# Narrowing 64-bit weight words on Trainium2: three instructions a block instead of four, with the sign carried by ScalarE's Prelu

## The chip, the core and the metric

The kernel runs on one core of one Trainium2 chip. A core has five engines with a queue of instructions each: TensorE (PE) for matrix products, VectorE (DVE), ScalarE (ACT) and GpSimd (POOL) for work on tiles, and SyncE (SP), which here issues the DMA transfers. Each engine takes its queue in order: an instruction that waits holds up all that stand behind it on the same engine. The metric is device time in microseconds of one execution; less is better.

## The reference

Three layers in a row, all in fp32 for the reader, with weights that reach the chip as 64-bit words (float64):

```
attention: B 4, H 8, S 576, D 64; a key is seen if 0 <= i - j < 64
x  = softmax(q k^T / 8, masked) v          -> 2304 x 512
g  = x @ w_gate; h1 = silu(g) * (x @ w_val)     512 -> 1536
x2 = h1 @ w_out                                1536 -> 512
h2 = (x2 @ w1) * (x2 @ w2)                      512 -> 1024
out = (h2 @ w3) @ w_out2                       1024 -> 1024 -> 512
```

## The kernel before

**Stages.** Attention takes 24 steps (about 10 to 107 us of the profiled execution); a step takes two groups of queries: S on PE (L400, L410), the maxima on DVE (L417), two groups of three Exp on ACT (L424), the reciprocal of the sums on DVE (L430, L431), the scaling on POOL (L434), the transposition on PE (L443) and its copy on DVE (L449), then P times V on PE (L463) and its copy on ACT (L477, L480). Stages follow each other in one program: the first gate (w_gate, w_val; to about 387), project (w_out, L691 ff., to about 540), the second gate (w1, w2; to about 717) and the final products.

**Matrix products.** Every operand is split in a high and a low part, and a product takes three passes (high x high, high x low, low x high). The gates multiply blocks of 768 tokens by seven products instead of eight; their weight operands (w_g_1h and so on) and token operands (xo_10 and so on) are sums of blocks, made by casts (L197), subtractions (L201) and combinations (L205). Project goes over three token parts of 768 (tp); in each over twelve blocks f of 128 rows of w_out; for every second f it needs two casts ph and two subtractions pl, of h that was stored to memory and loaded back. At the end of a tp, ACT and DVE copy the accumulators to X (L721, L724), which frees them for the next tp.

**Narrowing.** A load brings 128 x 1024 words of 64 bits into a tile `st` (two buffers: a third load waits for the first tile to be read). `narrow` (L176 to L193) makes an fp32 number of each word, 512 columns at a time, in four jobs: a (L185, DVE) shifts the low word right by 29; b (L187, DVE) takes the sign bit of the high word and joins it to that; c (L189, ACT) multiplies the high word, read as a float, by 2^-112, which moves its exponent to the range of fp32; d (L191, DVE) shifts the high word left by three and joins the low word. There are 38 loads, so 76 blocks. What follows makes operands of them, or (w_out, w_out2, w3) copies them (by_wo, by_z, by_w) for a store to memory (wo, zd, w3d), from which they are loaded again in fp32. The copies by_z and by_w share two buffers: a copy waits for the store before the last one.

**Order.** Nothing is scheduled at run time. A class `Plan` (L86 to L150) holds a list of jobs, each with the engines that may do it, a cost for each, and the jobs it needs. While the fixed work of a stage is written out, `advance` lets the plan's clock go on and puts each job on an engine's queue where its own reckoning finds a free time: a job can start when those that it needs are reckoned done. A load is reckoned landed `plan.landing` = 6.0 us after its issue (10.0 in the first two f of project). In attention, `during_attention` charges a step's fixed work as 2.9 us of DVE, 3.2 of ACT and 2.6 of POOL and then advances by 3.85. POOL takes no jobs after attention. SP's loads stand in the same kind of queue, and SP keeps eight transfers under way: the ninth is issued when one of them has landed.

Of the kernel before, what the change touches and what calls it, by code (L numbers as in the profile page):

```python
# [7 lines left out]
F32 = mybir.dt.float32  # L8
# [3 lines left out]
AF = mybir.ActivationFunctionType  # L12
ALU = mybir.AluOpType
# [19 lines left out]
def window_attention_moe_kernel(ctx: ExitStack, tc: tile.TileContext, q, k, v, w_gate, w_val, w_out, w1, w2, w3, w_out2, out):  # L33
# [118 lines left out]
    plan = Plan()  # L152
# [8 lines left out]
    def act(n):  # L161
        return 0.17 + 0.0009 * n

    def dve(n):
        return 0.16 + 0.00104 * n
# [6 lines left out]
    def halves(t):  # L172
        words = t.bitcast(I32).rearrange("p (n two) -> p n two", two=2)
        return words[:, :, 0], words[:, :, 1]

    def narrow(part, load):  # L176

        def low():
            return halves(part())[0]

        def high():
            return halves(part())[1]

        n = 512
        a = plan.job(lambda eng: eng.tensor_scalar(out=low(), in0=low(), scalar1=29, scalar2=None,  # L185
                                                   op0=ALU.logical_shift_right), [load], DVE=0.1 + 0.0006 * n)
        b = plan.job(lambda eng: eng.scalar_tensor_tensor(out=low(), in0=high(), scalar=-2 ** 31, in1=low(),  # L187
                                                          op0=ALU.bitwise_and, op1=ALU.bitwise_or), [a], DVE=dve(n))
        c = plan.job(lambda eng: eng.mul(out=high().bitcast(F32), in_=high().bitcast(F32), mul=2.0 ** -112),  # L189
                     [b], ACT=act(n))  # L190
        return plan.job(lambda eng: eng.scalar_tensor_tensor(out=high(), in0=high(), scalar=3, in1=low(),  # L191
                                                             op0=ALU.logical_shift_left, op1=ALU.bitwise_or),
                        [c], DVE=dve(n))  # L193

    def cast(hi, src, after, n, slots=1):
        def fn(eng):
# [17 lines left out]
    class Doubles:  # L214
# [15 lines left out]
        def narrowed(self):  # L230
            return [narrow(lambda j=j: self.st[:, 512 * j:512 * j + 512], self.loaded) for j in range(2)]
# [848 lines left out]
```

## Time and profile before

| | us |
|---|---|
| runs | 873.64, 871.74, 873.38 |
| median | 873.38 |
| span of the profiled execution, first to last instruction | 869.7 |
| PE busy | 839.7 (97%) |
| DVE busy | 582.2 (67%) |
| ACT busy | 421.2 (48%) |
| POOL busy | 86.2 (10%) |

The span is that of one profiled execution; of that execution the profile has the span alone, and the median of the runs is 3.7 us above it. A profile is read by stretch here: PE is busy nearly all the time, and the others are busy at other times, so the shares of the whole say little. Where PE stands idle, the row after the gap names who released it.

### The profile page before, as it was taken

What the parts mean: (1) busy time and instruction counts of PE and PEld (TensorE: products, weight loads), DVE (VectorE), ACT (ScalarE), POOL (GpSimd) and SP (SyncE); (2) the same over time, 40 slices, a digit from 0 to 9 for tenths busy, and PEclk for the clock granted to TensorE, in tenths of its full rate; (3) what the DMA queues carried; (4) which work ended last, traced back from release to release, by engine and by line L of the source; (5) the groups of instructions that cost most, each with busy time, mean ns of one, the idle gap of its engine ahead of it and who ended that gap; (6) DMA issues with size and microseconds to landing.
All of it is one profiled execution on the core that took longest, in us unless ns stands there. A gap on an engine that the chain in (4) does not pass through costs nothing.

```text
span 869.7 us, 14819 instructions
## 1 busy us (share of the span) xinstructions
PE 839.7 (97%) x5610; PEld 791.1 (91%) x5610; DVE 582.2 (67%) x1173; ACT 421.2 (48%) x1075; POOL 86.2 (10%) x119
## 2 busy tenths in 40 slices
PE   7899888899999999999989999999999999999998
PEld 6777687899999999999989999999999998888886
DVE  4899958878688768875797573867788644531400
ACT  6878855464646454733465442445454423430300
POOL 3678930000000000000000000000000000000000
PEclk9999999999999999999999999999999999999999
DMA  9979300135356323599987331023545179131511
GB/s 198 218 159 188 93 1 37 40 126 189 111 186 219 124 104 151 200 350 402 369 300 245 119 122 49 37 71 123 194 158 193 50 267 362 39 131 64 179 49 48
DMA packets 112535, 136.23 MB, mean 157 GB/s; under 512 B 61392, under 2 KB 78032, under 8 KB 111440
## 3 DMA queue, kind: packets, MB, share of 16 engines
q1 hardware_dynamic: 112320, 135.16, 47.6%
q8 instruction: 44, 0.72, 0.4%
q14 instruction: 27, 0.22, 0.1%
q10 hardware_dynamic: 144, 0.13, 0.0%
HBM read 92.27 MB, written 42.99 MB: 156 GB/s over the span
## 4 chain that ended last, share of the span: by engine, by line
PE 81%; DVE 7%; DMA 5%; ACT 2%; SPq 2%; issue 1%; POOL 1%; POOLq 0%; ACTq 0%; DVEq 0%
PE ala L578 14%; PE alb L578 14%; PE o L707 12%; PE out L818 11%; PE beb L578 7%; PE bea L578 7%; PE acc L774 5%; PE gab L578 3%; PE gaa L578 3%; DMA wo<-wo 2%; DMA zd<-by_z 2%; PE PV L463 1%; DVE ptt L449 1%; SPq L347 1%; DMA st_z<-in_moe_w_out_dram 1%
## 5 line engine op out<-in xcount | busy, mean ns | idle before, releaser
L707 PE MATMUL o<-ph,wo 128*128 128x384 f32 x576 | 147.7, 337 | 2.7 <-ACT X L721 2.7
L707 PEld LDWEIGHTS o<-ph,wo 128*128 128x128 f32 x576 | 105.0, 189 | 3.0 <-ACT X L721 3.0
L707 PE MATMUL o<-pl,wo 128*128 128x384 f32 x288 | 96.9, 336 | 0.0
L585 ACT COPY ha<-ala 128x384 f32<-128x384 f32 x90 | 42.9, 479 | 51.5 <-PE ala L578 50.3
L589 DVE TENSOR_TENSOR ha<-ha,bea 128x384 f32<-128x384 f32 x60 | 33.2, 553 | 45.0 <-PE bea L578 26.6
L707 PEld LDWEIGHTS o<-pl,wo 128*128 128x128 f32 x288 | 54.5, 189 | 0.0
L424 ACT ACTIVATE pexp<-S,stat 128x128 f32<-128x128 f32 x144 | 51.8, 392 | 0.0
L599 ACT ACTIVATE ha<-ha 128x384 f32<-128x384 f32 x54 | 28.4, 526 | 39.0 <-DVE ha L589 39.0
L434 POOL TENSOR_TENSOR pexp<-pexp,stat 128x384 f32<-128x384 f32 x48 | 44.4, 945 | 28.5 <-DVE stat L431 22.6
L836 DVE COPY o<-out 128x512 f32<-128x512 f32 x11 | 7.6, 692 | 57.7 <-PE out L818 57.7
L201 DVE TENSOR_TENSOR pl<-pl,ph 128x768 fp32r<-128x768 f32 x36 | 33.5, 956 | 16.5 <-ACT ph L197 16.1
L197 ACT CAST ph<-pl 128x768 fp32r<-128x768 f32 x36 | 29.3, 835 | 31.1 <-DMA pl<-h 24.1
L585 ACT COPY c12b<-alb 128x384 f32<-128x384 f32 x30 | 14.5, 482 | 48.7 <-PE alb L578 48.6
L833 ACT COPY o<-out 128x512 f32<-128x512 f32 x6 | 3.5, 588 | 65.5 <-PE out L818 65.5
L589 DVE TENSOR_TENSOR c22b<-c22b,beb 128x384 f32<-128x384 f32 x30 | 16.6, 554 | 26.4 <-ACT c22b L585 26.3
L424 ACT ACTIVATION_READ_ACCUMULATOR pexp<-S,stat 128x1 f32 x144 | 33.1, 230 | 0.0
L417 DVE TENSOR_REDUCE stat<-S 128x3 f32<-128x384 f32 x48 | 24.3, 546 | 8.2 <-PE S L410 8.0
L463 PEld LDWEIGHTS PV<-ptt,v 128*64 128x64 f32 x576 | 19.5, 137 | 10.2 <-DVE ptt L449 5.7
L463 PE MATMUL PV<-ptt,v 128*64 128x64 f32 x576 | 22.9, 227 | 6.1 <-DVE ptt L449 5.0
L578 PE MATMUL ala<-xo,w_g_1h 128*128 128x384 f32 x120 | 26.9, 337 | 1.7 <-ACT w_g_1h L197 1.7
L201 DVE TENSOR_TENSOR xo<-X,xo 128x384 fp32r<-128x384 f32 x37 | 22.6, 641 | 5.7 <-ACT xo L197 5.7
L201 DVE TENSOR_TENSOR fl<-fl,fh 128x768 fp32r<-128x768 f32 x24 | 21.7, 952 | 6.9 <-ACT fh L197 6.9
(490 smaller groups left out, 2407.4 us busy)
## 6 DMA issues: line engine op xcount, KB each, us to landing
h<-ha SPq DMA_DIRECT2D x60, 384.0 KB, 3.2
pl<-h SPq DMA_DIRECT2D x36, 384.0 KB, 6.7
fl<-h SPq DMA_DIRECT2D x24, 384.0 KB, 6.1
st_w<-in_moe_w_dram SPq DMA_DIRECT2D x8, 1024.0 KB, 6.9
st_g<-in_moe_w_gate_dram SPq DMA_DIRECT2D x6, 1024.0 KB, 5.5
st_v<-in_moe_w_val_dram SPq DMA_DIRECT2D x6, 1024.0 KB, 5.4
st_wo<-in_moe_w_out_dram SPq DMA_DIRECT2D x6, 1024.0 KB, 5.8
wo<-by_wo SPq DMA_DIRECT2D x12, 512.0 KB, 3.9
```

What stands on the lines that cost most here:

```text
L197: (eng.copy if eng is nc.scalar else eng.tensor_copy)(out=hi(), in_=src())
L201: return plan.job(lambda eng: eng.tensor_tensor(out=lo(), in0=src(), in1=hi().bitcast(F32), op=ALU.subtract), after, slots=slots, DVE=dve( ...
L424: nc.scalar.activation(out=pe[:, jj, :], in_=so[:, jj, :], func=AF.Exp, bias=st[:, 0, x, jj:jj + 1], accum_out=st[:, 1, x, jj:jj + 1])
L434: nc.gpsimd.tensor_tensor(out=pe, in0=pe, in1=st[:, 3, x, :].unsqueeze(2).to_broadcast([P, SUB, P]), op=ALU.mult)
L463: nc.tensor.matmul(pp[64 * h:64 * h + 64, 64 * (SUB * x + jj):64 * (SUB * x + jj) + 64], lhsT=vt[u][e][:, at, h, :], rhs=t[:, x, jj, c:c + ...
L578: nc.tensor.matmul(acc, lhsT=self.wt.ops[p, x][:, m, :], rhs=self.xs.ops[p, m][:, y, :], start=start and n == 0, stop=n == 5, skip_group_c ...
L585: nc.scalar.copy(out=out, in_=src)
L589: nc.vector.tensor_tensor(out=out, in0=x, in1=y, op=ALU.add)
L599: nc.scalar.activation(out=h, in_=src, func=func)
L707: nc.tensor.matmul(acc[m, x], lhsT=wos.tiles[i // 6][:, i % 6, :], rhs=rows[2 * tp + x].words(f, b), start=f == n == 0, stop=f == NF - 1 a ...
L774: nc.tensor.matmul(acc, lhsT=w3T[i][c // 3][:, x, (c % 3) * P:(c % 3) * P + P], rhs=zt[c, y], start=c == n == 0, stop=c == NI - 1 and n == 2)
L818: nc.tensor.matmul(acc, lhsT=rows[blk].words(i, x)[:, t * P:t * P + P], rhs=w34[i][y], start=i == n == 0, stop=i == NI - 1 and n == 2)
```

## The change

Job b no longer works on DVE and no longer waits for a. It is one Prelu on ACT, on the high word read as a float: the word is multiplied by 2^-112, and where it is negative also by -2^32, which makes it positive and puts 32 into its exponent. The last shift left by three then moves that exponent bit to the place of the sign. Job d needs both a and b. So the multiplication (c) and the join of the sign (b on DVE) become one instruction on ACT.

```
-        b = plan.job(lambda eng: eng.scalar_tensor_tensor(out=low(), in0=high(), scalar=-2 ** 31, in1=low(),
-                                                          op0=ALU.bitwise_and, op1=ALU.bitwise_or), [a], DVE=dve(n))
-        c = plan.job(lambda eng: eng.mul(out=high().bitcast(F32), in_=high().bitcast(F32), mul=2.0 ** -112),
-                     [b], ACT=act(n))
+        b = plan.job(lambda eng: eng.activation(out=high().bitcast(F32), in_=high().bitcast(F32), func=AF.Prelu,
+                                                scale=2.0 ** -112, alpha=-2.0 ** 32), [load], ACT=act(n))
         return plan.job(lambda eng: eng.scalar_tensor_tensor(out=high(), in0=high(), scalar=3, in1=low(),
                                                              op0=ALU.logical_shift_left, op1=ALU.bitwise_or),
-                        [c], DVE=dve(n))
+                        [a, b], DVE=dve(n))
```

Since the plan reckons with other costs and other needs, jobs of all kinds come to stand at other places. Three places on ACT follow; the numbers in a name tell tiles of one kind apart, and differ between the programs for the same tile.

ACT in attention, from the Exp of one step to those of the next, before (st_g is the first weight tile, stat the step's maxima and sums, pexp the Exp):

```order
L424 ACTIVATE pexp_456,stat_443<-S_387,stat_443 128x128 x3
L424 ACTIVATE pexp_517,stat_443<-S_389,stat_443 128x128 x3
L385 ACTIVATE qT_531<-T_0_488 128x288
L385 ACTIVATE qT_531<-T_1_492 128x288
L480 COPY X_0_454<-PV_496 128x192
L480 COPY X_1_535<-PV_496 128x192
L424 ACTIVATE pexp_537,stat_521<-S_469,stat_521 128x128 x3
L189 ACTIVATE st_g_310<-st_g_310 128x512
L424 ACTIVATE pexp_601,stat_521<-S_471,stat_521 128x128 x3
L387 COPY kT_615<-T_3_572 128x288
```

and now (st_v is the second weight tile):

```order
L424 ACTIVATE pexp_456,stat_443<-S_387,stat_443 128x128 x3
L189 ACTIVATE st_g_310<-st_g_310 128x512 x2
L424 ACTIVATE pexp_518,stat_443<-S_389,stat_443 128x128 x3
L385 ACTIVATE qT_532<-T_0_489 128x288
L385 ACTIVATE qT_532<-T_1_493 128x288
L480 COPY X_0_454<-PV_497 128x192
L480 COPY X_1_536<-PV_497 128x192
L424 ACTIVATE pexp_538,stat_522<-S_470,stat_522 128x128 x3
L189 ACTIVATE st_v_460<-st_v_460 128x512
L424 ACTIVATE pexp_605,stat_522<-S_472,stat_522 128x128 x3
```

Both steps on st_g moved ahead of a group of Exp in the earlier step, and the first one on st_v, which stood some steps later, came between the two groups of the next.

ACT in project, at the operands of f = 6 (ph_0_3, ph_1_3), before (st_z is a tile of w_out2, by_z its copies):

```order
L189 ACTIVATE st_z_4673<-st_z_4673 128x512 x2
L197 CAST by_z_0_5001<-st_z_4673 128x512
L197 CAST by_z_1_5004<-st_z_4673 128x512
L189 ACTIVATE st_z_4743<-st_z_4743 128x512 x2
L197 CAST ph_0_3_5069<-pl_0_3_4989 128x768
L197 CAST ph_1_3_5072<-pl_1_3_4991 128x768
L197 CAST by_z_0_5076<-st_z_4743 128x512
L197 CAST by_z_1_5078<-st_z_4743 128x512
```

and now:

```order
L197 CAST ph_0_2_4924<-pl_0_2_4779 128x768
L197 CAST ph_1_2_4928<-pl_1_2_4781 128x768
L189 ACTIVATE st_z_4665<-st_z_4665 128x512 x2
L197 CAST by_z_0_4964<-st_z_4645 128x512
L197 CAST by_z_1_4967<-st_z_4645 128x512
L197 CAST by_z_0_5002<-st_z_4665 128x512
L197 CAST ph_0_3_5032<-pl_0_3_4958 128x768
L197 CAST ph_1_3_5035<-pl_1_3_4960 128x768
L197 CAST by_z_1_5039<-st_z_4665 128x512
```

The first copy of the second tile, by_z_0, stood behind ph_0_3 and ph_1_3 and now stands ahead of them.

ACT at the end of project's first token part, before (st_w is a tile of w3, by_w its copies, X the copies of the accumulators):

```order
L197 CAST ph_0_0_5284<-pl_0_0_5208 128x768
L197 CAST ph_1_0_5290<-pl_1_0_5210 128x768
L189 ACTIVATE st_w_5217<-st_w_5217 128x512 x2
L881 COPY by_w_0_5328<-st_w_5217 128x512
L881 COPY by_w_1_5330<-st_w_5217 128x512
L197 CAST ph_0_1_5364<-pl_0_1_5286 128x768
L197 CAST ph_1_1_5366<-pl_1_1_5288 128x768
L721 COPY X_0_0_4921<-o_0_1_4926 128x384
L721 COPY X_0_1_4922<-o_1_1_4928 128x384
```

and now:

```order
L189 ACTIVATE st_w_5142<-st_w_5142 128x512 x2
L197 CAST ph_0_0_5252<-pl_0_0_5173 128x768
L197 CAST ph_1_0_5254<-pl_1_0_5175 128x768
L881 COPY by_w_0_5257<-st_w_5142 128x512
L881 COPY by_w_1_5260<-st_w_5142 128x512
L189 ACTIVATE st_w_5216<-st_w_5216 128x512 x2
L197 CAST ph_0_1_5323<-pl_0_1_5248 128x768
L197 CAST ph_1_1_5326<-pl_1_1_5250 128x768
L881 COPY by_w_0_5329<-st_w_5216 128x512
L881 COPY by_w_1_5332<-st_w_5216 128x512
L721 COPY X_0_0_4885<-o_0_1_4890 128x384
L721 COPY X_0_1_4886<-o_1_1_4892 128x384
```

A second tile of w3 now stands with its narrowing and its copies ahead of the copies X; before, one tile did.

## Rows read from the trace of the kernel before

**Rows 1.** The page, totals of each engine and the line on project's subtraction.
```profile
span 869.7 us, 14819 instructions
...
PE 839.7 (97%) x5610; PEld 791.1 (91%) x5610; DVE 582.2 (67%) x1173; ACT 421.2 (48%) x1075; POOL 86.2 (10%) x119
...
L201 DVE TENSOR_TENSOR pl<-pl,ph 128x768 fp32r<-128x768 f32 x36 | 33.5, 956 | 16.5 <-ACT ph L197 16.1
```

**Rows 2.** Stretches: us; busy PE, PEld, DVE, ACT, POOL; clock, DMA share, GB/s.
```profile
80.00:100.00 20.00, 18.27 (x310) 14.90 (x311) 19.53 (x43) 17.53 (x82) 18.70 (x26) 1.00 0.67 161
180.00:200.00 20.00, 20.00 (x117) 20.00 (x116) 13.49 (x30) 11.20 (x26) 0.00 (x0) 1.00 0.36 127
400.00:420.00 20.00, 20.00 (x117) 20.00 (x116) 11.05 (x17) 7.11 (x10) 0.00 (x0) 1.00 1.04 406
```

**Rows 3.** Waits of PE: who was waited for, us in total, times, longest.
```profile
PE o L707 <- ACT X L721: 2.7, 1, 2.7
...
PE ala L578 <- ACT w_g_1h L197: 1.7, 1, 1.7
...
PE beb L578 <- DVE w_b_3h L201: 0.5, 1, 0.5
```

**Rows 4.** Line 187: duration ns min/median/max, first and last start.
```profile
L187 DVE SCALAR_TENSOR_TENSOR st_g<-st_g x12: 652/686/691, 23.5 to 332.9; 128x512 int32<-128x512 int32 x12
L187 DVE SCALAR_TENSOR_TENSOR st_v<-st_v x12: 684/689/1257, 45.1 to 354.9; 128x512 int32<-128x512 int32 x12
```

**Rows 5.** ACT in order of time: start, us, line, tiles, [idle before].
```profile
27.85 0.39 ACT L424 ACTIVATE pexp<-S,stat 128x128 f32<-128x128 f32 x1
...
49.22 0.70 ACT L189 ACTIVATE st_v<-st_v 128x512 f32<-128x512 f32 x1
```

**Rows 6.** Line 499, ACT's first table load.
```profile
L499 ACT ACT_TABLE_LOAD  x1: 1283/1283/1283, 0.8 to 0.8; - x1
```

**Rows 7.** SP's queue in order of time, around 27 us.
```profile
26.80 0.59 SPq L227 DMA_DIRECT2D st_v<-in_moe_w_val_dram  x1
```

**Rows 8.** DMA issues from 26.5 to 27.2: KB, median us to landing.
```profile
st_v<-in_moe_w_val_dram SPq DMA_DIRECT2D x1, 1024.0 KB, 6.4
```

**Rows 9.** DVE in order of time, in attention.
```profile
29.73 0.16 DVE L430 TENSOR_SCALAR stat<-stat 128x6 f32<-128x6 f32 x1
...
30.36 1.30 DVE L191 SCALAR_TENSOR_TENSOR st_g<-st_g 128x512 int32<-128x512 int32 x1
...
37.42 1.01 DVE L417 TENSOR_REDUCE stat<-S 128x3 f32<-128x384 f32 x2
...
40.87 1.01 DVE L417 TENSOR_REDUCE stat<-S 128x3 f32<-128x384 f32 x2
```

**Rows 10.** PE in order of time, two places where it waited.
```profile
115.48 0.62 PE L578 MATMUL ala<-xo,w_g_6h 128*128 128x384 f32 x2 [0.43 <-DVE xo L201]
...
439.73 0.44 PE L707 MATMUL o<-ph,wo 128*128 128x384 f32 x1 [2.70 <-ACT X L721]
```

**Rows 11.** DVE in order of time, before the gate's second weight block.
```profile
160.44 1.29 DVE L187 SCALAR_TENSOR_TENSOR st_g<-st_g 128x512 int32<-128x512 int32 x2
```

**Rows 12.** ACT in order of time, in project.
```profile
410.42 0.84 ACT L197 CAST ph<-pl 128x768 fp32r<-128x768 f32 x1 [0.21 <-DMA pl<-h]
411.94 0.66 ACT L197 CAST by_z<-st_z 128x512 fp32r<-128x512 f32 x1 [0.68 <-DMA zd<-by_z]
...
435.13 1.29 ACT L189 ACTIVATE st_w<-st_w 128x512 f32<-128x512 f32 x2 [2.44 <-DVE st_w L187]
436.58 1.25 ACT L881 COPY by_w<-st_w 128x512 f32<-128x512 f32 x2 [0.17 <-DVE st_w L191]
...
439.21 1.61 ACT L721 COPY X<-o 128x384 f32<-128x384 f32 x4
```

**Rows 13.** SP's queue in order of time, the second load of w3.
```profile
433.66 0.63 SPq L227 DMA_DIRECT2D st_w<-in_moe_w_dram  x1
```

**Rows 14.** DMA issues from 424 to 425: KB, median us to landing.
```profile
st_w<-in_moe_w_dram SPq DMA_DIRECT2D x1, 1024.0 KB, 8.3
```

## The prediction

> **What bounds the kernel now.** I read the totals first, then busy time by stretch, then what TensorE (PE) waited for, then the rows of ScalarE (ACT), VectorE (DVE) and the queue of SyncE (SP) at the places where the new program has another order. The totals [rows 1] say that PE is busy for 839.7 us of 869.7; so at most 30 us are to be had, and only where PE stands idle. The stretches [rows 2] say where that is. From 180 us on PE is busy 20.00 of 20 nearly everywhere, with ACT at 7 to 11: an instruction taken from DVE there is worth nothing by itself. In 80 to 100, inside attention, DVE is the fullest engine, 19.53 of 20, and PE 18.27. The waits [rows 3] name the rest: 1.7 us for ACT's cast of w_g_1h, 0.5 for w_b_3h, and one wait of 2.7 us for ACT's copy of X, at the end of project's first token part. So the change is worth something at four places: attention, the start of the gate stage, the end of the second gate stage, and project, where ACT is waited for.
>
> **The change, part by part.** Removed: 76 instructions at L187 (38 loads of two blocks). One takes 0.69 us, and up to 1.257 in attention, where GpSimd (POOL) works too [rows 4]: 76 x 0.69 = 52 us of DVE, nearly all of it under a full PE. Put in place of the multiplication: 76 Prelu of the same tile on ACT. The multiplication took 0.70 [rows 5]; I take the same for Prelu. What hides a difference is ACT's slack, 9 to 13 us of 20 behind 180 us [rows 2]; at twice the time Prelu would still fit there, and in attention four of them would cost up to 4 x 0.7 = 2.8. Less than nothing it can't be, since it has as many elements.
>
> A table switch is a price to exclude. Loading ACT's table takes 1283 ns here [rows 6]. By the order Prelu now stands between Exp in three places of attention; with a table of its own it would need six loads, 6 x 1.283 = 7.7 us on ACT. The built program has two loads, at the same lines as before, so I put this at nothing. [...]
>
> What moves matters more. In the old chain the ACT step came third, behind two DVE steps, and the planner put it late. Now Prelu needs only the load, so the planner, which reckons a landing 6 us after the time at which *it* issues the load, puts it early on ACT. If the load is later than that, ACT waits, and everything queued on ACT behind it waits too.
>
> *Attention.* The first order excerpt shows the Prelu of st_v between the two groups of Exp of one step. That load was issued at 26.80 [rows 7] and took 6.4 us [rows 8], so it landed at 33.2; the old multiplication of it came at 49.22 [rows 5]. The SP queue has the load in the same place in both programs, behind the same transfers, so it lands at 33.2 again. The second group of Exp ran from 27.85 [rows 5]. Now ACT would stand from about 27.5 to 33.2, then Prelu 0.7 to 33.9, three Exp in about 1.05 to 34.95. DVE's L430, which needs both groups' sums, ran at 29.73 [rows 9] and would run at 35.0. Behind it on DVE stand kT, ptt and the next L417; POOL's scaling, PE's transposes of P and PV follow: attention is set back by 35.0 - 29.73 = 5.3 us.
>
> Part of that comes back, because DVE has less to do in the steps. Gone are four L187 (0.65 to 1.26 each [rows 4], 3.7 us in all), and two L191 (1.30 each, [rows 9]) now run while ACT stands. By the order, DVE also does three 128x256 subtractions fewer and two combinations more. Not all is won, since a step needs some 3.5 us however little DVE has to do: 37.42 to 40.87 [rows 9] is 3.45. I summed the larger of 3.6 and 2.35 plus the side work over the steps behind the stall: 84.1 before, 81.5 after, 2.6 less. The same sum over all 20 steps is some 5 us above what the trace shows, so it is dear; I take 2.3 back, with bounds 0 (a step is set by PE) and 4.3 (all by DVE). Attention: +3.0, from +1.0 to +5.3.
>
> *Start of the gate stage.* Side work of attention ends some steps earlier, so xo_61 is ready when PE comes to it, and the 0.43 at 115.48 goes [rows 10]. At 160.44 DVE has two L187 for 1.29 us [rows 11] ahead of L191, the ACT cast and PE's wait of 1.7 [rows 3]. Both Prelu now run long before; L191 can start at 160.44, and the cast comes about 1.6 earlier. I take 1.5 of the 1.7 and 0.3 of a later half microsecond: -2.2 together (-1.0 to -2.7). What is late next there are the sums of xo between 130 and 152, whose order is unchanged. At the other gate stage st_b is narrowed about 10 us sooner, and the 0.5 for w_b_3h goes [rows 3]: -0.5 (0 to -0.5).
>
> *Project, f = 6.* The second excerpt shows ACT's cast by_z standing ahead of the casts ph_0_3 and ph_1_3 that PE needs; before, it stood behind them. It needs a buffer that the store zd frees; it started at 411.94, waiting for zd [rows 12], and the DMA engines are full there (1.04, [rows 2]), so it can't be earlier. Then ph_0_3 and ph_1_3 follow at 412.6 and 413.4 (0.84 each), where the second started at 410.42 before [rows 12], and DVE's last subtraction (0.956, [rows 1]) ends near 415.2. PE reaches f = 6 at about 412 (it stops at 437.03 after six more f of 4.1 to 4.2) and wants that operand at 412.7: 2.5 us.
>
> *Project, end of the first token part.* The third excerpt: a second load of w3 (st_w), its two Prelu and its two by_w copies now stand ahead of X L721. Before, PE restarted at 439.73, 2.70 after it stopped [rows 10], on X at 439.21 [rows 12]. The second w3 load was issued at 433.66 [rows 13]; now it stands ahead of two loads of pl and I take 429.7, the end of a landing that frees its place in SP's queue. At 8.3 us [rows 14] it lands at 438.0. Then two Prelu (1.29), two ph (0.84 each, piped 1.57), two by_w (1.25), all from [rows 12], and the first copy of X (1.61 / 4 = 0.4) is done at 438.0 + 1.3 + 1.55 + 1.25 + 0.4 = 442.5, against 439.7: +2.8. The 2.5 of f = 6 lies inside this, because X waits for transfers that don't wait for PE. Bounds: 0.5 (the load lands 2.3 sooner) and 5.4 (both stalls add). [...]
>
> Sum: +3.0 - 2.2 - 0.5 + 2.8 = **+3.1 us**. Span 869.7 + 3.1 = 872.8. The median of the runs, 873.38, lies 3.7 above the span; I take that as fixed: **876.5**.
>
> **The rivals.** *The waits are refunded (faster).* If what stands behind the blocked Prelu runs in a rush once it is free, since S and the maxima of the next step are done by then, the following steps could give back all 4.3 and 0.5 to 1 more; with a w3 load that lands early the sum is 5.3 - 4.8 - 2.2 - 0.5 + 0.5 = -1.7, or 871.7. For it: DVE was at 19.5 of 20, so its lost work counts in full. Against it: steps alternate between PE and DVE, and nothing in the rows shows a step under 2.8 us. *It evens out (no change).* Attention +1.5, project +1.2, the gains 2.7: 0, or 873.4. *Both stalls in full (much slower).* No return in attention, +5.3, both project stalls adding, +5.4, the start of the gate -1.9: +8.8, or 882. The stalls of ACT decide between these: the change is slower from the point where they cost more than 1.7 above the 5 to 7 us of DVE work, gate waits and steps that are won. *The change doesn't do what it says.* L187 is gone from the program in all 76 places; only a table load hidden in Prelu would bring this, +7.7, and it has about no chance.
>
> **How the numbers follow.** Forecast 0.50 (876.5, its own range 874.5 to 879.5); evens out 0.22; refunded 0.16; in full 0.12. A measurement here tells a change from none at about 0.2%, 1.75 us. Slower 0.62, same 0.22, faster 0.16. The range takes the lower edge of the refunded case and most of the full one: 871.3 to 881.
>
> **What would show it.** Right: ACT idle for 5 to 6 us up to about 33 with the load of st_v as releaser; L430 of that step at 35; L187 absent; no PE wait for w_g_1h; PE waits at f = 6 on pl or ph, and a wait for X of more than 2.7 that ends at 441 to 443. Wrong: ACT's wait at 27 absent or below 2 us (the load lands sooner, or the Prelu got behind Exp); attention over no later than in the old program; a wait for X that is no longer; a table load beside a Prelu.

## The result, and the profile after

The changed kernel is slower: 882.6 us (median of four, 882.3 to 882.9) against 873.0, a ratio of 1.0117 with a 95% interval of 1.0088 to 1.0146. The profiled execution has a span of 881.0 against 869.7. Slower was forecast, at 876.5 and at most 881: the sign holds, the size doesn't; it is three times the +3.1 that the sum gave.

The totals first (the page of the changed kernel; they answer to [rows 1]):

```profile
span 881.0 us, 14789 instructions
...
PE 844.7 (96%) x5610; PEld 795.3 (90%) x5610; DVE 535.4 (61%) x1095; ACT 419.1 (48%) x1078; POOL 85.0 (10%) x118
```

DVE is busy for 46.8 us less, near the 52 that the prediction gave for L187, and the kernel is 11.3 longer. PE has the same 5610 matrix products and is busy 5.0 us more: some of them ran slower. Where that is, the part on why the prediction was right or wrong shows.

What PE waited for (who was waited for: us in total, times, longest):

```profile
PE o L707 <- ACT X L721: 4.5, 1, 4.5
PE PT L443 <- ACT pexp L424: 4.1, 1, 4.1
PE T L373 <- DVE ptt L449: 3.8, 3, 2.7
...
PE bea L578 <- DVE xo L201: 2.7, 2, 1.7
...
PE bea L578 <- DVE w_g_6h L201: 1.5, 1, 1.5
...
PE beb L578 <- DVE w_b_3h L201: 0.6, 1, 0.6
...
PE o L707 <- DVE pl L201: 0.6, 1, 0.6
...
PE o L707 <- ACT ph L197: 0.3, 1, 0.3
```

Against [rows 3]: the wait for X is 4.5 instead of 2.7, the one for w_g_1h is gone and one of 1.5 for w_g_6h stands in its place, the one for w_b_3h has stayed, and two in attention are new, 4.1 for an Exp and 2.7 for DVE's ptt.

The first of these (ACT in order of time, the last bracket is idle time before and what ended it; it answers to [rows 5]):

```profile
26.96 0.39 ACT L424 ACTIVATE pexp<-S,stat 128x128 f32<-128x128 f32 x1
...
33.30 0.67 ACT L189 ACTIVATE st_v<-st_v 128x512 f32<-128x512 f32 x1 [5.87 <-DMA st_v<-in_moe_w_val_dram]
33.88 0.34 ACT L424 ACTIVATE pexp<-S,stat 128x128 f32<-128x128 f32 x1
```

ACT stands for 5.87 us with the Prelu of st_v at the head of its queue, until the load lands at 33.3, and the Exp behind it comes at 33.88, six us after the 27.85 of before. DVE's L430, behind those Exp, ran at 35.03 (29.73 in [rows 9]):

```profile
35.03 0.17 DVE L430 TENSOR_SCALAR stat<-stat 128x6 f32<-128x6 f32 x1 [5.06 <-ACT pexp L424]
```

The second wait of attention (DVE, and then POOL, in order of time):

```profile
70.07 0.19 DVE L431 RECIPROCAL stat<-stat 128x6 f32<-128x6 f32 x1
73.76 0.69 DVE L201 TENSOR_TENSOR w_v_3h<-st_v,w_v_3h 128x256 fp32r<-128x256 f32 x1 [3.50 <-POOL w_v_3h L197]
74.38 1.01 DVE L449 COPY ptt<-PT 128x384 f32<-128x384 f32 x2
```

```profile
70.43 1.61 POOL L434 TENSOR_TENSOR pexp<-pexp,stat 128x384 f32<-128x384 f32 x2 [2.62 <-DVE stat L431]
71.99 0.60 POOL L362 COPY v<-v 64x512 f32<-64x512 f32 x1
72.65 0.61 POOL L363 COPY v<-v 64x512 f32<-64x512 f32 x1
73.33 0.40 POOL L197 CAST w_v_3h<-st_v 128x256 fp32r<-128x256 f32 x1
```

DVE's subtraction for w_v_3h stands ahead of ptt, which PE needs, and waits for POOL's cast. That cast stands on POOL behind the scaling of P, which itself had waited for DVE's reciprocal at 70.07, and behind two copies of v. So DVE hands over at 70.26 and does nothing for 3.50 us, and PE waits for it during the last 2.7.

The table gives the time of four events in each profiled execution: the maxima (L417) of attention's 7th and 24th step on DVE, and PE's first and last product of project (L707). The ratios are of the timed runs, each against runs of the kernel before that were taken beside them.

| kernel | ratio, 95% interval | 7th step | 24th step | project, first | last | span |
|---|---|---|---|---|---|---|
| before | 1 | 32.5 | 104.9 | 386.9 | 541.1 | 869.7 |
| changed | 1.0117, 1.0088 to 1.0146 | 38.5 | 111.0 | 394.1 | 552.2 | 881.0 |
| e1 old order | 0.9955, 0.9941 to 0.9969 | 33.2 | 102.3 | 384.4 | 538.4 | 867.0 |
| e2 attention old | 1.0000, 0.998 to 1.002 | 31.9 | 102.1 | 382.4 | 537.3 | 866.3 |
| e3 attention new | 1.0082, 1.0065 to 1.01 | 38.4 | 114.8 | 394.5 | 548.5 | 877.2 |
| e4 project new | 1.0007, 0.999 to 1.0025 | 33.2 | 104.9 | 387.0 | 544.8 | 873.4 |
| e5 wait only | 1.0045, 1.0022 to 1.0068 | 37.2 | 106.0 | 388.2 | 541.9 | 870.4 |
| e6 cast on ACT | 1.0046, 1.0017 to 1.0075 | 38.2 | 108.9 | 389.4 | 547.0 | 875.8 |
| e7 late landing | 1.0005, 0.9986 to 1.0024 | 32.5 | 102.1 | 382.5 | 540.8 | 869.2 |
| e8 old attention, old project | 0.9957, 0.9939 to 0.9975 | 31.3 | 102.7 | 384.0 | 537.8 | 866.5 |
| e9 filled, wrong place | 1.0063, 1.0034 to 1.0092 | 37.7 | 111.1 | 393.2 | 544.7 | 873.2 |
| e10 wait only again | 1.0030, 1.0013 to 1.0047 | 37.8 | 107.8 | 388.4 | 542.0 | 870.5 |
| e11 late all | 0.9984, 0.9964 to 1.0003 | 33.7 | 103.4 | 384.3 | 539.6 | 868.0 |
| e12 filled | 1.0047, 1.0026 to 1.0068 | 36.2 | 107.6 | 389.7 | 541.3 | 869.9 |

The changed kernel against the one before: +6.1 at the end of attention, +7.2 at the start of project, +11.1 at its end, and no more behind it. One profiled execution is not the median: single runs of one kernel lie up to 9 us apart here (the kernel before 866.0 to 874.8 in 31 runs), so a table row tells *where*, and the ratio tells *how much*.

### The profile page after: what moved, and what is told of

It reads as the page before. It is cut to its first block, busy times and chain, and to the rows that moved or that the text cites. A ratio compares the mean times of both kernels' runs of the same rounds, so it can differ in the third digit from the quotient of the medians.

```text
span 881.0 us, 14789 instructions
## 1 busy us (share of the span) xinstructions
PE 844.7 (96%) x5610; PEld 795.3 (90%) x5610; DVE 535.4 (61%) x1095; ACT 419.1 (48%) x1078; POOL 85.0 (10%) x118
## 4 chain that ended last, share of the span: by engine, by line
PE 81%; DVE 6%; DMA 5%; SPq 3%; ACT 3%; issue 1%; POOL 1%; ACTq 0%; DVEq 0%; POOLq 0%
PE ala L578 14%; PE o L707 13%; PE alb L578 13%; PE out L818 11%; PE beb L578 7%; PE bea L578 6%; PE acc L774 5%; PE gab L578 3%; PE gaa L578 3%; DMA zd<-by_z 2%; SPq L347 2%; DMA pl<-h 1%; PE PV L463 1%; DVE ptt L449 1%; DMA st_w<-in_moe_w_dram 1%
## 5 line engine op out<-in xcount | busy, mean ns | idle before, releaser
L707 PE MATMUL o<-ph,wo 128*128 128x384 f32 x576 | 148.5, 337 | 4.7 <-ACT X L721 4.5
L707 PEld LDWEIGHTS o<-ph,wo 128*128 128x128 f32 x576 | 105.5, 190 | 5.4 <-ACT X L721 4.8
L707 PE MATMUL o<-pl,wo 128*128 128x384 f32 x288 | 97.2, 338 | 0.6 <-DVE pl L201 0.6
L589 DVE TENSOR_TENSOR ha<-ha,bea 128x384 f32<-128x384 f32 x60 | 33.2, 553 | 60.7 <-PE bea L578 33.6
L707 PEld LDWEIGHTS o<-pl,wo 128*128 128x128 f32 x288 | 54.8, 190 | 1.2 <-DVE pl L201 1.2
L434 POOL TENSOR_TENSOR pexp<-pexp,stat 128x384 f32<-128x384 f32 x48 | 43.5, 927 | 33.7 <-DVE stat L431 26.1
L589 DVE TENSOR_TENSOR c22b<-c22b,beb 128x384 f32<-128x384 f32 x30 | 16.6, 553 | 29.6 <-ACT c22b L585 29.5
L201 DVE TENSOR_TENSOR xp<-X,xp 128x384 fp32r<-128x384 f32 x42 | 21.8, 552 | 13.2 <-ACT xp L197 13.2
L417 DVE TENSOR_REDUCE stat<-S 128x3 f32<-128x384 f32 x48 | 24.3, 547 | 8.5 <-PE S L410 8.2
L197 ACT CAST xp<-X 128x384 fp32r<-128x384 f32 x42 | 19.8, 514 | 18.0 <-PE o L707 16.1
L443 PE MATMUL PT<-ident,pexp 128*128 128x128 f32 x144 | 23.1, 298 | 4.4 <-ACT pexp L424 4.1
L578 PE MATMUL ala<-xo,w_g_5l 128*128 128x384 f32 x78 | 25.4, 360 | 1.9 <-ACT xo L197 1.6
L585 ACT COPY c11b<-alb 128x384 f32<-128x384 f32 x30 | 14.4, 479 | 26.9 <-PE alb L578 26.9
## 6 DMA issues: line engine op xcount, KB each, us to landing
h<-ha SPq DMA_DIRECT2D x60, 384.0 KB, 3.4
pl<-h SPq DMA_DIRECT2D x36, 384.0 KB, 7.9
fl<-h SPq DMA_DIRECT2D x24, 384.0 KB, 5.8
```

Source lines behind the costliest of these rows:

```text
L197: (eng.copy if eng is nc.scalar else eng.tensor_copy)(out=hi(), in_=src())
L201: return plan.job(lambda eng: eng.tensor_tensor(out=lo(), in0=src(), in1=hi().bitcast(F32), op=ALU.subtract), after, slots=slots, DVE=dve( ...
L417: nc.vector.tensor_reduce(out=st[:, 0, x, :], in_=sc[2 * m + x], op=ALU.max, axis=AX.X, negate=True)
L434: nc.gpsimd.tensor_tensor(out=pe, in0=pe, in1=st[:, 3, x, :].unsqueeze(2).to_broadcast([P, SUB, P]), op=ALU.mult)
L578: nc.tensor.matmul(acc, lhsT=self.wt.ops[p, x][:, m, :], rhs=self.xs.ops[p, m][:, y, :], start=start and n == 0, stop=n == 5, skip_group_c ...
L585: nc.scalar.copy(out=out, in_=src)
```

## The experiments

All but e9 to e12 were made to take apart three things that the change does at once: DVE loses 76 instructions, ACT's first step no longer waits for DVE's, and by that the plan sets another order in attention, in the gate and in project. The edits are shown with lines broken, and `x and f()` written as `if x: f()`.

**e1 to e4: work taken away, and order moved.** e1 keeps a job of L187's cost in the plan, which emits nothing, so every instruction but L187 stands where it stood:

```
+        gap = plan.job(lambda eng: None, [a], DVE=dve(n))
         b = plan.job(lambda eng: eng.activation(..., func=AF.Prelu, scale=2.0 ** -112, alpha=-2.0 ** 32),
-                     [load], ACT=act(n))
+                     [gap], ACT=act(n))
```

> Prelu in place of the multiplication and no L187, but every instruction on every engine stands in the order of the kernel before: the plan still reckons with the removed step, which emits nothing. Theory (the time was lost by the moved order, the removed DVE work itself is a gain): 2 to 4 us faster than before, about 870; attention ends 1 to 2.5 us earlier, the wait for w_g_1h (1.7) is gone, PE restarts in project 0.5 to 1 earlier. Rival (Prelu or its sign trick costs time by itself): 876 or more. Rival (DVE work is worth nothing under PE): 873, no change.

Measured: 0.9955, 3.9 us faster, span 867.0. As the theory said in sum, and not where it said. 2.6 is won in attention (24th step at 102.3). At the start of the gate nothing is won. Waits of PE in e1:

```profile
PE o L707 <- ACT X L721: 2.1, 1, 2.1
...
PE ala L578 <- ACT w_g_1h L197: 1.7, 1, 1.7
```

The wait for w_g_1h is 1.7 as before, with both L187 gone. DVE and then ACT in e1:

```profile
159.97 0.56 DVE L589 TENSOR_TENSOR ha<-ha,bea 128x384 f32<-128x384 f32 x1 [1.94 <-PE bea L578]
160.44 1.29 DVE L191 SCALAR_TENSOR_TENSOR st_g<-st_g 128x512 int32<-128x512 int32 x2
...
161.16 0.44 ACT L197 CAST w_g_1h<-st_g 128x256 fp32r<-128x256 f32 x1
```

On DVE L191 stands behind L589, which waits for a product of PE, and the cast of w_g_1h needs L191. Without L187 DVE is merely idle for longer (1.94) ahead of L589, and the cast comes at the same place. The wait for X is 0.6 shorter.

e2 has `gap` for the two loads of attention only, so attention is in the old order and the rest in the new; e3 has it for all but those two; e4 for all but the tiles of w_out2 and w3:

```
+        gap = plan.job(lambda eng: None, [a], DVE=dve(n)) if name in ("g0", "v0") else load
```

> The changed kernel, with attention alone in the order of the kernel before. Theory (the new kernel's +11.2 is 6.0 from two waits in attention, 1.2 at the start of the gate with its slower clock, 3.9 in project): the 6.0 goes and 1 to 2 more is won in attention, what is left is 3 to 4 slower than before, about 876 to 877. Rival (the loss of attention is given back or taken later anyway, because project's transfers set the end): 881 to 883.

> The reverse: attention in the new order, everything behind it in the order of the kernel before. Theory: attention 6.0 later, and up to 2 won behind it: 877 to 879, with ACT's wait of 5.9 for the load of st_v and DVE's wait of 3.5 for POOL's cast w_v_3h. Rival (project alone decides): 873.

> The order of the kernel before up to project, the new order for the tiles of w_out2 and w3 (st_z, st_w) alone. Theory: project 3.9 longer, against 2 to 3 won before it: 874 to 875, with a wait of PE for X of about 4.5 and half a microsecond at f = 6. Rival (the long wait for X comes only because the gate ended its own transfers later): 870 to 871, the wait for X as before, 2.7.

Measured: e2 1.0000, e3 1.0082, e4 1.0007. Against e1, which is the same work in the old order, attention's new order costs 1.27% (e3), about 11 us, and project's 0.52% (e4), 4.5 us. e2 - e1 is 0.45% for gate and project together, so the gate's new order costs nothing within the intervals. These add up: -0.45 + 1.27 + 0.45 = 1.27%, where the changed kernel has 1.17. e2 came out better than expected (876 to 877, which is 1.003 to 1.005): without attention's loss, the win of e1 and the loss of project cancel. e4 is near what was expected, by its time; its wait for X is longer than the 4.5 expected, and the wait at f = 6 isn't there. PE at the end of its first token part, in e4:

```profile
442.68 0.69 PE L707 MATMUL o<-ph,wo 128*128 128x384 f32 x1 [5.57 <-ACT X L721]
```

The prediction had 442.5 for this restart, worked out for a PE that comes to the place at the same time as before; in e4 it does. In the changed kernel it was 450.38 after 4.46, with a PE that came later. That e4 agrees to 0.2 us is in part luck, as ACT shows:

```profile
437.15 1.27 ACT L189 ACTIVATE st_w<-st_w 128x512 f32<-128x512 f32 x2 [1.83 <-DMA st_w<-in_moe_w_dram]
439.27 0.83 ACT L197 CAST ph<-pl 128x768 fp32r<-128x768 f32 x1 [0.85 <-DMA pl<-h]
440.30 0.83 ACT L197 CAST ph<-pl 128x768 fp32r<-128x768 f32 x1 [0.20 <-DMA pl<-h]
```

The load landed 0.9 sooner than the 438.0 of the sum, and the two ph then waited 1.05 for pl, which the sum didn't have.

**e5, e10: the first wait by itself.** e1 with one instruction more, which nothing reads:

```
                 so, (m, x) = sc.pop(n), divmod(n, 2)
+                if n == 9: nc.scalar.copy(out=own.tile([P, 1], F32, name="peek"),
+                                          in_=halves(left1[0, 1].st[:, :1])[1].bitcast(F32))
```

> The kernel of e1 (old order, no L187) with one more instruction: a copy of one column of st_v on ACT, ahead of the second group of Exp of the sixth step, where the changed kernel has its Prelu. So ACT waits there for that load, and nothing else is moved. Theory (the wait is a loss by itself): step seven is 5 to 6 us later than in e1; 1 to 2.5 of it come back in later steps, and a PE clock at half speed behind the gap costs 1 to 3 more: 4 to 6 us slower than e1, about 872 to 874 where before is 871.5. Rival (the steps behind the wait catch up): within 1.5 of e1.

> e5 once more, beside e9 on the same chip. Theory: 0.3 to 0.8% above before, as e5 (ratio 1.0045), with 3.4 to 6.8 us of half clock behind PE's gap of 3.9. Rival (e5 was high by chance, and the wait is worth only what its profiled execution showed, 3.4 against e1): ratio 0.999 to 1.001.

Measured: 1.0045 and 1.0030, against e1's 0.9955: 0.75 to 0.9%, 6.5 to 8 us by the timed runs. ACT in e5:

```profile
32.66 0.19 ACT L421 COPY peek<-st_v 128x1 f32<-128x1 f32 x1 [4.92 <-DMA st_v<-in_moe_w_val_dram]
32.76 0.36 ACT L424 ACTIVATE pexp<-S,stat 128x128 f32<-128x128 f32 x1
```

A copy of 128 x 1 that takes 0.19 us makes the kernel 6.5 us slower or more, because it waits for 4.92 and the Exp stand behind it. In the profiled executions the 7th step is 4.0 and 4.6 later than in e1 and the 24th 3.7 and 5.5: next to nothing comes back. That speaks against the refund, and for a price that is nearly the wait itself. The spans are only 3.4 and 3.5 longer than e1's; the timed runs lose more, and their mean granted clock is lower too (0.986 to 0.994 in e5 and 0.988 to 0.994 in e10, 0.992 to 0.998 in e1). The Exp need nothing of st_v, and stood for those 4.92 us all the same, as their place in ACT's queue has it.

**e6: the second wait.** The changed kernel with one cast moved from POOL to ACT:

```
                 a = cast(lambda p=p: self.place(p, 0), lambda p=p: self.words(*at[p]), after, n)
+                if self.name == "v0" and p == 3: a.cost.pop("POOL")
```

> The changed kernel with the cast of w_v_3h of the first pair taken from POOL and put on ACT; the place of DVE's subtraction that needs it is the same. Theory: DVE's wait of 3.5 us at 70 is gone, and with it PE's gap of 2.7 and the half clock behind it: 3 to 5 faster than the changed kernel, ratio to before about 1.007. Rival (POOL's own delay sets these steps, whoever makes the cast): no faster.

Measured: 1.0046, 0.7% or about 6 us faster than the changed kernel (the intervals allow 1 to 11). DVE at that place:

```profile
73.25 0.68 DVE L201 TENSOR_TENSOR w_v_3h<-st_v,w_v_3h 128x256 fp32r<-128x256 f32 x1 [1.38 <-ACT w_v_3h L197]
```

The wait is 1.38 instead of 3.50, not gone, and what went is worth more than the 2.1 us of difference: from the 11th to the 24th step e6's profiled execution takes 52.5, the changed kernel's 56.5. A part of that is PE's clock, which fell to 0.50 at 75.9 in the changed kernel, behind the 2.7 us of PE's wait, and stayed at 1.00 from 70 to 82 in e6. The price of 6 us is uncertain for the same reason: e6's runs fall in two groups, 872.1 to 873.0 (granted clock 0.994) and 875.7 to 879.6 (0.983 to 0.990).

**e7, e11: the plan's reckoning of landings.** Here the order is mended at its cause; e11 adds the tiles of project:

```
-            self.loaded = loading(fn, before, lag=plan.landing)
+            self.loaded = loading(fn, before, lag=plan.landing + 6.0 * (self.name == "v0"))          # e7
+            self.loaded = loading(fn, before, lag=plan.landing + (6.0 if self.name == "v0" else
+                4.0 if self.name[:2] == "w3" or self.name[0] == "z" else 0.0))                       # e11
```

> The changed kernel, where the plan reckons the landing of the second weight load (st_v) 6 us later, so that its Prelu stands three steps later on ACT. Theory: ACT's wait of 5.9 is gone, and with it both of PE's clock drops around 35; attention ends 5 to 8 earlier than in the changed kernel; what is left over before is project's part: 872 to 876, ratio 1.000 to 1.004. Rival (the second wait, for POOL, takes over the loss): ratio above 1.007.

> The changed kernel, where the plan reckons the landing of st_v 6 us later (as e7) and those of the tiles of w_out2 and w3 4 us later: by_z stands behind the operands of PE again, and one tile of w3 instead of two is ahead of X. Theory (all of the loss is Prelu put ahead of loads that land later than reckoned): attention as in e7, 2 to 3 earlier than before, the gate as in e2, PE's wait for X 2.7 or less instead of 5: ratio 0.992 to 0.996, better than both kernels. Rival (project is set by its transfers, wherever ACT's steps stand): as e7, 1.000.

Measured: e7 1.0005, e11 0.9984. Six us more in one number of the plan take away 1.1%, the whole loss of attention; the second wait went with the first, since w_v_3h got another place. ACT no longer waits for the load of st_v, and the 24th step is at 102.1, where e2 with the old attention has it. e11 was expected at 0.992 to 0.996 and missed that. PE's restart in project:

```profile
438.54 0.69 PE L707 MATMUL o<-ph,wo 128*128 128x384 f32 x1 [2.90 <-ACT X L721]
```

The wait for X is 2.90 (2.7 or less was expected), where e7 has 5.6: one tile of w3 less ahead of X. From the first to the last product of project e11 takes 155.3, e7 158.3, and before 154.2. That part went as the theory said. But by_z kept its place ahead of ph at f = 6 (a wait of 0.56 for pl is left), and the intervals of e7 and e11 overlap. So the mend in project is shown in the trace and not by the times.

**e8: the best of them.** The old order in attention and for the tiles of project, the new one in the gates.

> Attention and the tiles of w_out2 and w3 in the old order, the gate stages in the new one: what e2 won at the start of the gate and e1 in project together. Theory: 1 to 2 faster than e1 (ratio 0.9955), so a ratio of 0.993 to 0.995. Rival (what e2 won at the gate's start was a clock that did not drop in that execution, not the order): as e1.

Measured: 0.9957, the same as e1. The gate's new order by itself is worth nothing that the times show, as the rival said. e1 and e8 are both faster than the kernel before by 0.4%, and than the changed one by 1.6%.

**e9, e12: what the gap costs behind itself.** e5 with 27 transposes of the identity on PE, whose result nothing reads. e9 had them one step too late:

```
                     po = bank(f"PT{2 * m + x}")[:, :SUB * P].rearrange("p (j k) -> p j k", j=SUB)
+                    [nc.tensor.transpose(po[:, 0, :], ident, ident) for _ in range(27 * (m == 4 and x == 1))]
```

> The kernel of e5, in which ACT waits for st_v, with 27 more transposes of the identity on PE, into the bank that the transposes of P overwrite next: work without use, put where PE stood idle for 3.9 us. Theory (part of what a wait costs is the half clock that PE gets behind it): the idle gap is filled, no half clock from 32 to 39 as e5 had it for 6.8 us, and 1 to 3 us faster than e5 in the same call. Rival (the clock behind the gap costs nothing, since the steps there are set by DVE): the same as e5, within 0.5.

They ran at 39.6, behind the gap, which stayed at 4.24: this one tells nothing of the question. It tells that 3.1 us of PE work in a step are not all hidden: the 7th to the 11th step took 18.8 us, 16.9 in e10. In e12 they stand in the gap:

> As e9, with the 27 transposes of the identity one step earlier, between the two groups of transposes of P where PE in fact stood idle in e9 and e10 (they go to columns of the first group's bank that nothing reads). Theory (part of a wait's price is the half clock behind PE's gap): PE is busy for 3.1 to 3.9 of the gap, so the gap is under 1.5 us, there is no half clock between 30 and 40 (6.8 us in e5 and e10), and step eleven is 0.7 to 2 earlier than in e10 (54.7 there); ratio 1.000 to 1.002 against 1.003 and 1.0045. Rival (the clock behind the gap costs nothing): step eleven at 54.5 to 55, ratio 1.003 to 1.0045.

Stretches in e10 and then in e12 (from and to, us, busy us of PE, PEld, DVE, ACT, POOL, granted clock of PE, DMA share, GB/s):

```profile
32.00:36.00 4.00, 1.30 (x5) 1.04 (x5) 1.38 (x4) 2.69 (x14) 0.85 (x2) 0.50 1.31 245
36.00:40.00 4.00, 4.00 (x59) 3.35 (x59) 3.63 (x9) 3.02 (x14) 3.08 (x4) 0.66 1.36 211
```

```profile
32.00:36.00 4.00, 3.33 (x45) 2.53 (x44) 2.58 (x6) 3.90 (x18) 2.04 (x3) 1.00 1.37 221
36.00:40.00 4.00, 3.79 (x66) 3.00 (x64) 3.97 (x9) 3.93 (x19) 3.51 (x6) 1.00 0.99 171
```

Both executions wait for the same load. In e10 PE stands idle, the clock is at 0.50 behind the gap, and from 36 to 40 PE is busy all the time with 59 products; in e12, at a granted clock of 1.00, it gets through 66 and is not even full. The 11th step is at 53.0, and at 54.7 in e10: 1.7 earlier, the size that the theory gave. But most of this isn't the clock. ACT in e10 and then in e12, where the load lets it go on:

```profile
33.31 0.19 ACT L421 COPY peek<-st_v 128x1 f32<-128x1 f32 x1 [5.62 <-DMA st_v<-in_moe_w_val_dram]
```

```profile
32.10 0.19 ACT L421 COPY peek<-st_v 128x1 f32<-128x1 f32 x1 [4.62 <-DMA st_v<-in_moe_w_val_dram]
```

The load landed 1.2 sooner in e12. From there to the 7th step e12 takes 4.1 and e10 4.5, and from the 7th to the 11th both take 16.8 to 16.9. So at most half a microsecond can be the clock's, and the theory isn't confirmed. The whole kernel is no faster either: 1.0047. In its profiled execution PE waited for a load of q at 68, the clock fell to 0.50 from 71.7 on, and by the 24th step e12 is level with e10. What the clock costs elsewhere, other executions show; it is told below.

## Why the prediction was right or wrong

The sum failed in these steps: attention's +3.0 left out a second wait (+6.1 measured), the start of the gate's -2.2 was put down to L187 (+1.1), PE's clock had no term at all, and the wait at f = 6 was taken to lie inside the wait for X, where the two add up (+3.9 instead of +2.8). The stages below go by the profiled executions.

**The first wait in attention: right, to a tenth.** Landing 33.2, found 33.3; ACT idle 5 to 6, found 5.87; L430 at 35.0, found 35.03. The order and one landing time were enough. The tenth is luck: the load was issued at 27.58 and not at 26.80, and took 5.7 instead of 6.4. Of the return, 2.3 was taken; the changed kernel's delay against the old one goes from 6.0 at the 7th step to 3.2 at the 11th (54.5 against 51.3), 2.8 back. In e1, which has no such wait, DVE's lighter steps alone gain 1.8 over the same four steps, and in e5 and e10, where DVE had nothing less to do than in e1, by the 24th step 0.3 had come back in the one and 0.9 more was lost in the other: so the return is DVE's lighter steps, as the prediction had it, and no rush behind the wait. The refunded case falls.

But the return isn't sure, and this the prediction didn't have. e3 has the changed kernel's order on all engines up to 145 us, and its load landed at 33.1. Stretches of the changed kernel and then of e3:

```profile
36.00:40.00 4.00, 4.00 (x61) 3.05 (x60) 3.97 (x9) 3.21 (x15) 3.49 (x5) 0.71 1.33 215
40.00:44.00 4.00, 3.96 (x65) 3.26 (x66) 4.00 (x8) 3.78 (x18) 3.04 (x4) 1.00 0.78 171
```

```profile
36.00:40.00 4.00, 4.00 (x43) 3.02 (x43) 3.97 (x10) 3.00 (x15) 3.44 (x6) 0.50 1.36 208
40.00:44.00 4.00, 4.00 (x46) 3.44 (x46) 3.08 (x5) 2.91 (x15) 2.93 (x4) 0.50 0.69 150
```

The half clock behind the gap ended at 38.4 in the changed kernel's execution, at 40.0 in e6 (the same order up to there) and at 44.6 in e3. From the 7th to the 11th step they took 16.0, 18.1 and 20.1 us: with the longest half clock nothing of the wait came back.

**The second wait in attention: missed, and the costliest miss.** The prediction counted what DVE has to do in each step, and took for granted that it could do it when its turn came. One of these jobs, the subtraction for w_v_3h, needs a cast that the plan had put on POOL, behind a scaling that waits for DVE. It is in the order of the changed program, on DVE's and POOL's queues; the prediction read only ACT's queue for instructions that wait. From the 14th to the 15th step (75.3 against 66.5) attention was set back from +5.2 to +8.8, of which 2.7 came back by the end; the 2.0 before that, from +3.2 at the 11th step, came mostly in the 13th, where DVE has three jobs on st_v, 2.8 us, ahead of ptt. e6 puts the price of the wait at about 6 us, and not closely. The step of the sum that failed is "Attention: +3.0", with bounds of 1.0 to 5.3; it was +6.1 in the profiled execution, and 11 by e3 against e1, which also holds e1's own win there (2.6).

**The start of the gate: -2.2 was forecast, +1.1 came.** Two steps failed. First, the wait for w_g_1h was ascribed to L187. e1 takes L187 away and the wait stays; it goes only where the order moved, and then one of 1.5 for w_g_6h comes. Second, the clock was left out. Stretches of the changed kernel:

```profile
136.00:140.00 4.00, 2.75 (x8) 2.10 (x9) 4.00 (x10) 2.23 (x6) 0.00 (x0) 0.67 0.00 0
140.00:144.00 4.00, 4.00 (x14) 4.00 (x13) 1.89 (x4) 3.36 (x8) 0.00 (x0) 0.50 0.00 0
144.00:148.00 4.00, 4.00 (x24) 4.00 (x24) 3.05 (x7) 1.95 (x4) 0.00 (x0) 0.98 0.42 165
```

From 140 to 144 PE is busy all the time and does 14 products, from 144 to 148 it does 24. The gaps ahead of it (1.7 and 1.1, waits for xo that the kernel before has as well) are the old ones; the clock behind them stayed at 0.50 for longer here, and fell to it once more at 158. In the kernel before it is at 0.61 from 132 to 136 and back at 0.96 in the next four. From the 24th step to project the changed kernel takes 283.1 us, with 10.2 of them at half clock, and the one before 282.0, with 3.4. Among the executions with 3.4 the new order is the faster: 280.4 to 281.3 (e6, e7, e8, e11) against 282.0 to 282.2 (before, e1, e4, e5, e9, e12). So the order won some 0.7 to 1.8 in the traces, a part of the 2.2, though e8's times don't show it, and the longer half clock of this execution took it back.

**The clock: put at nothing, without a reason.** "At most 30 us are to be had, and only where PE stands idle" takes PE's busy time as fixed. It isn't: the same 5610 products took 5.0 us more, and PE was busy at half clock for 23.8 us in the changed kernel's execution, at 25, 35, 76, 137, 158 and 448, and for 10.1 in the one before, at 48, 133 and 440. The timed runs show it too: the granted clock is 0.984 to 0.990 in the four runs of the changed kernel and 0.988 to 1.000 in 31 runs of the kernel before. It isn't the whole loss: the changed kernel's run at 0.990 took 882.3, and the six of the kernel before at 0.990 took 872.1 to 874.1.

**The second gate stage: wrong, -0.5 was 0.** The wait for w_b_3h is 0.6 as before: that st_b is narrowed earlier did not move what w_b_3h waits for.

**Project: the mechanism right at X, the parts off.** +2.8 was forecast, 3.9 measured (from the first to the last product 154.2 before, 158.1 now), 4.5 by e4 against e1. ACT there:

```profile
445.98 1.26 ACT L189 ACTIVATE st_w<-st_w 128x512 f32<-128x512 f32 x2 [2.87 <-DMA st_w<-in_moe_w_dram]
447.13 1.68 ACT L197 CAST ph<-pl 128x768 fp32r<-128x768 f32 x2
448.72 1.24 ACT L881 COPY by_w<-st_w 128x512 f32<-128x512 f32 x2
449.87 0.46 ACT L721 COPY X<-o 128x384 f32<-128x384 f32 x1
```

It is the chain of the sum, link by link: the second tile of w3, its two Prelu, two ph, two by_w, X. The wait at f = 6 was given as 2.5 and was 0.28 + 0.56, and PE lost 1.6 there against the kernel before. The wait for X grew by 1.8 (4.46 against 2.70, answering to [rows 10]). So f = 6 doesn't lie inside X, as the sum had it: the two add up. The loads of that stretch (issues of DMA, KB each, median us from issue to landing, 425 to 450):

```profile
DMA packets 3413, 9.40 MB, mean 376 GB/s; under 512 B 266, under 2 KB 2029, under 8 KB 3037
...
st_w<-in_moe_w_dram SPq DMA_DIRECT2D x3, 1024.0 KB, 8.6
```

The second tile of w3 took 8.6 (437.33 to 445.96) where the sum had 8.3 from [rows 14], and 7.6 in e4. The transfers of this stretch moved 376 GB/s. The rest of the 3.9 is the clock behind the longer gap; the changed kernel and then the one before:

```profile
448.00:452.00 4.00, 1.62 (x5) 1.62 (x6) 3.95 (x8) 4.00 (x9) 0.00 (x0) 0.50 1.00 384
452.00:456.00 4.00, 4.00 (x18) 4.00 (x17) 4.00 (x9) 4.00 (x9) 0.00 (x0) 0.65 1.02 365
```

```profile
440.00:444.00 4.00, 4.00 (x15) 4.00 (x15) 4.00 (x9) 3.55 (x9) 0.00 (x0) 0.57 0.98 256
```

Both fall to half clock: PE is busy at it for 4.4 us in the changed kernel and for 3.4 in the one before, and the difference is worth only 0.4 to 0.5. What the whole of it is worth, e2 shows, whose gap was 3.58 and whose clock stayed up:

```profile
437.55 0.44 PE L707 MATMUL o<-ph,wo 128*128 128x384 f32 x1 [3.58 <-ACT X L721]
...
438.00:442.00 4.00, 4.00 (x25) 4.00 (x25) 3.91 (x9) 4.00 (x10) 0.00 (x0) 1.00 1.08 403
```

It did 25 products in four us where the kernel before did 15, and behind the gap it gained 1.6 us on it.

**Prelu itself: right.** It took 671 to 680 ns where the multiplication took 674 to 687 (medians of line 189, st_g, st_v and st_w), by tile from 9 ns less (st_v) to 6 more (st_g). That it can't be less, with as many elements, was the author's estimate and isn't shown. ACT has its two table loads as before:

```profile
L499 ACT ACT_TABLE_LOAD x1 | 1.3, 1283 | 0.8 <-PEq L1064 0.8
L539 ACT ACT_TABLE_LOAD x1 | 1.3, 1283 | 0.0
```

**The DVE work taken away: 3.9 us of 52 (e1), nearly all in attention,** as "nearly all of it under a full PE" had it. This gain is in the changed kernel too, and is lost three times over.

**The range.** The measured 882.6 lies above its end, 881. It was built from the stalls that had been found; none of its cases held a wait that had been overlooked, though the same kind had been found twice by reading one queue of three, and none held the clock. The "in full" case (882) met the number by luck: it had +5.3, -1.9 and +5.4 for attention, gate and project, and the profiled execution has +6.1, +1.1 and +3.9. Nor was the 3.7 between span and median fixed: it is 1.6 in the changed kernel, so the spans are 11.3 apart and the medians 9.6.

## What to carry to other kernels

When a change takes a dependency away, read what now stands at the head of each queue and for what it waits, on all engines and not only on the one that got the new instruction: the 52 us of DVE work that were removed gave 4, and two instructions that came to stand ahead of others cost some 6 each. A planner that reckons landings from its own clock needs a margin for a queue that is behind: 6 us on one load took the loss of attention away. And where an engine's clock falls behind a gap, price the gap at more than its length, and as a range: behind the wait for X 3.4 us of half clock cost 1.6, and one order of attention gave 16.0 to 20.1 us for the same four steps.

## What the runs showed of the hardware that was not expected

PE's clock behind gaps: after gaps of 1.1 to 4.6 us the granted clock was at 0.50 in some executions and not in others, and how long differed for the same order: 3.4 us behind the gap at 31 in the changed kernel, 10.2 in e3. One execution, e2's, shows no fall before its last half microsecond, with a gap of 3.58 in it.

This accounts for most of the spread of single runs. In the 31 runs of the kernel before, the 14 with a mean granted clock of 0.996 or more took 866.0 to 871.3, mean 868.9, and the 8 with 0.990 or less 872.0 to 874.8, mean 873.4; the correlation of time and clock is -0.93. What sets the clock of a run was not tried.
